# Scale vectors spread by GpSimd instead of the PE, and q of the third batch turned by the PE

## The chip, the cores and the metric

The kernel runs on one core of one Trainium2 chip. The metric is the device time of one execution in microseconds. Engines by the profile's names: PE (TensorE, matrix products, with PEld for its weight loads), DVE (VectorE), ACT (ScalarE), POOL (GpSimd), SP (SyncE, which here only starts DMA transfers). A "q" after an engine's name (ACTq, SPq) means its queue of DMA issues.

## The reference

Grouped attention over 8 batches (16 query heads that share 4 key heads, 384 positions, 64 per head), whose output goes into a residual MLP with per-channel scales:

```python
scores = scale * np.matmul(q, k.transpose(0, 1, 3, 2))      # k, v repeated 4x along heads
attn = softmax(scores)
x = matmul(attn, v)                                         # [8, 384, 1024] after a transpose
a1 = alpha1 * x + beta1
tok = np.einsum('ts,bsd->btd', w_tok, a1)
u = x + lam * tok
a2 = alpha2 * u + beta2
ch = np.maximum(a2 @ w_ch1, 0.0) @ w_ch2                    # 1024 -> 4096 -> 1024
out = u + lam * ch
```

alpha1, beta1, alpha2, beta2 and lam are vectors of 1024 numbers, one for each channel. Where channels lie along the free dimension, the kernel needs each vector copied to all 128 partitions. It keeps four such copies in `vecs`: alpha1 times lam (`g1`), beta1 times lam (`h1`), alpha2 (`al2`) and lam (`lam_t`).

## The kernel before

The eight batches go through a pipeline. `side(b)` is the attention of a batch, the product with w_tok and the turn of the result; `main(b)` is its MLP, in two parts: the first product (`h`, 32 column blocks) and the second (`ch`). The attention of batch b + 1 is cut into pieces and put between the matrix products of `main(b)`, at numbered places (`turns` for the first part, the second dictionary for the second). The attention of batch 0 has nothing to hide behind: it stands alone at the start ("the first batch" below).

```python
        def q_transpose(p, n=2, tag="tp", eng="DVE"):     # PE turns q of two pairs of heads
            src = qrs[1][:, 2 * p:2 * (p + n)] if b else qgs[2 * p // G][...]
            ...
            for i in range(n * NST):
                nc.tensor.matmul(out=ps[:, i, :], lhsT=src[:, i * P:(i + 1) * P], rhs=ident_f if f else ident,
                                 is_transpose=True, ...)
            evac(eng)(out=qT[:, p:p + n].rearrange("p a j s -> p (a j) s"), in_=ps)

        def scores(i, later=False):                       # q k^T, then exp on ACT
            sc = bank([P, 2, 4, P], "sc", "sc") if first else three()
            ...
                if first:                                 # the first batch's exponentials lie in hT
                    e = hTf[:, i % 6 * 1024:(i % 6 + 1) * 1024].rearrange("p (h k s) -> p h k s", h=2, k=4)
                nc.scalar.activation(out=e, in_=sc, func=EXP, scale=scale_qk)

        def av_piece(p, hh):
            ...
            nc.vector.tensor_tensor(out=x[...], in0=av[:, :, :, :D], in1=rinv.to_broadcast([P, 2, NST, D]), op=MUL)
            if first:
                a1s[p] = hTf[:, 6144 + p % 3 * S:6144 + (p % 3 + 1) * S].rearrange("p (a d) -> p a d", a=NST)
                nc.vector.tensor_tensor(out=a1s[p], in0=x[:, :, cols(p)], in1=bc(g1, p), op=MUL)
                return

        def spread(ps_, vs, tag, eng="DVE"):              # PE copies rows to all partitions
            ...
            for i, p in enumerate(ps_):
                nc.tensor.matmul(out=ps[:, i * w:(i + 1) * w], lhsT=sel[:, p:p + 1].to_broadcast([P, P]),
                                 rhs=rows_b[:, vs[0] * P:vs[1] * P], start=True, stop=True)
            evac(eng)(out=vecs[...], in_=...)
```

A float32 row goes through `spread` as three bf16 parts whose sum it is; `split` makes the parts on DVE (a cast, a difference, twice over). In the first batch, `beta1` enters the product with w_tok by a small extra product with two helper matrices `R` and `H` (`rows_r` and `fill_h`), and `fill_h` needs the split row.

The steps of the first batch stand in a table: after scores group i come the listed pieces (`ut` is the turn of the result for the MLP).

```python
        at = {0: [(warmup, 3), (scale_rows, 0), (split, 0, 1, 0)], 1: [(k_transpose, 1, 1), (split, 0, 1, 1)],
              2: [(q_transpose, 2, 2, "av")], 3: [(warmup, 1), (spread, lower, (0, 1), "tp")],
              4: [(av, 0)], 5: [(wtok_transpose, 0, "av"), (wtok_transpose, 1, "tp")],
              6: [(av, 1), (wtok_transpose, 2, "av"), (k_transpose, 2, 2, "tp")], 7: [(q_transpose, 4, 2, "av"), (scale_rows, 1), (split, 1, 2)],
              8: [(fill_h, 0), (rows_r, "tp"), (av, 2)], 9: [(spread, upper, (0, 1), "av", "ACT"), (q_transpose, 6, 2, "mm")],
              10: [(tok, 0)],
              11: [(av, 3)], 12: [(tok, 1), (ut, 0)], 13: [(av, 4), (tok, 2)], ...}
```

Loads: the vectors come from SP's queue, the weights from POOL's (w_ch1 in a ring of five chunks):

```python
        for t in (stage[:, 2120:2824], rows_b, sel):
            nc.vector.memset(t, 0.0)
        load_row(0, moe_alpha1); load_row(3, moe_lam); load_k(0, [2]); load_row(1, moe_beta1) ...
        ...
        load_v(0)
        nc.gpsimd.dma_start(out=wtok_in, ...)
        load_q4(2)
        load_q4(3)
        place_k(0, 0, (0,))
        for c in range(RING):
            load_w1(c)
        place_k(0, 1)          # k of the second pair of key heads to bf16, on POOL
```

The q and k of batch 2 and later are turned by DMA transposes (`flip_k`, `flip_q`), those of batch 2 from ACT's queue late in the first part of `main(1)`:

```python
                moves = [(0, 46 + 4 * i, flip_q, 2, 2 * i - 2, 2) if i else (0, 46, flip_k, 2) for i in range(5)]
```

The softmax here doesn't subtract the row's maximum and nothing guards it: scores larger than these inputs give would overflow.

Of the kernel before, what the change touches and what calls it, by code (L numbers as in the profile page):

```python
# [12 lines left out]
def kernel(  # L13
# [27 lines left out]
    ADD = mybir.AluOpType.add  # L41

# [74 lines left out]
    def flip_queue(b):  # L117
        return nc.scalar if b == 2 else nc.sync

    def flip_k(b):  # L120
        flip_queue(b).dma_start_transpose(out=kT.rearrange("p st h s -> p (st h) s"),
                                    in_=k2s[b].rearrange("p st h a d -> p (st h a d)"))

    def flip_q(b, i=0, n=NP):
        flip_queue(b).dma_start_transpose(out=qT[:, i:i + n].rearrange("p a j s -> p (a j) s"),
                                    in_=qrs[b][:, 2 * i:2 * (i + n)].rearrange("p h st d -> p (h st d)"))
# [16 lines left out]
    def bank(shape, tag, name, dtype=f32):  # L143
        if tag == "mm":
            return mms.tile(shape, dtype, tag="mm", name=name, bufs=2)
        return psum.tile(shape, dtype, tag=tag, name=name, bufs=2 if tag == "sc" else 1)

    def three():
        return threes[0].tile([P, 2, 4, P], f32, tag="sc", name="sc", bufs=3)
# [24 lines left out]
    def side(b):  # L174
# [22 lines left out]
        def q_transpose(p, n=2, tag="tp", eng="DVE"):  # L197
            src = qrs[1][:, 2 * p:2 * (p + n)] if b else qgs[2 * p // G][:, 2 * p % G:2 * p % G + 2 * n]
            src = src.rearrange("p h st d -> p (h st d)")
            f = src.dtype == f32  # L200
            ps = bank([P, n * NST, P], tag, "tp", src.dtype)
            for i in range(n * NST):
                nc.tensor.matmul(out=ps[:, i, :], lhsT=src[:, i * P:(i + 1) * P], rhs=ident_f if f else ident,  # L203
                                 is_transpose=True, start=(i == 0), stop=(i == n * NST - 1), skip_group_check=True)
            evac(eng)(out=qT[:, p:p + n].rearrange("p a j s -> p (a j) s"), in_=ps)
# [33 lines left out]
        def av_piece(p, hh):  # L239
# [20 lines left out]
            if first:  # L260
                a1s[p] = hTf[:, 6144 + p % 3 * S:6144 + (p % 3 + 1) * S].rearrange("p (a d) -> p a d", a=NST)
                nc.vector.tensor_tensor(out=a1s[p], in0=x[:, :, cols(p)], in1=bc(g1, p), op=MUL)
                return
# [3 lines left out]
            nc.vector.tensor_tensor(out=a1s[p], in0=t, in1=bc(h1, p), op=ADD)  # L267

# [40 lines left out]
        def rows_r(tag):  # L309
            ps = bank([P, 512], tag, "r")  # L310
            for st in range(NST):
                nc.tensor.matmul(out=ps[:32, :S], lhsT=ones, rhs=wtokT[:, st, :], start=(st == 0),
                                 stop=(st == NST - 1))
            turned = ps[:, S:S + 2 * NP].rearrange("p (i n) -> p i n", i=2)
            for i, c in enumerate((2, 4)):
                nc.tensor.matmul(out=turned[:, i], lhsT=rows_f[:NP, c * P:(c + 1) * P], rhs=ident_f[:NP, :NP],
                                 is_transpose=True, start=True, stop=True, skip_group_check=True)
            t = hTf[:32, 7296:7296 + S]
            nc.scalar.copy(out=t, in_=ps[:32, :S])
            nc.vector.scalar_tensor_tensor(out=R[:32], in0=t, scalar=masks[2], in1=ps[:32, :S], op0=MUL, op1=ADD)  # L320
            nc.vector.tensor_copy(out=al2T, in_=turned[:, 0])
            nc.vector.tensor_copy(out=a2T[:, :, S:S + 1], in_=turned[:, 1, :, None])


        def spread(ps_, vs, tag, eng="DVE"):
            n = len(ps_)
            ps = bank([P, 4, P], tag, "vec")
            w = vs[1] - vs[0]
            for i, p in enumerate(ps_):
                nc.tensor.matmul(out=ps[:, i * w:(i + 1) * w], lhsT=sel[:, p:p + 1].to_broadcast([P, P]),  # L330
                                 rhs=rows_b[:, vs[0] * P:vs[1] * P], start=True, stop=True)
            evac(eng)(out=vecs[:, vs[0]:vs[1], ps_[0] * P:(ps_[-1] + 1) * P].rearrange("p v (n d) -> p n v d", n=n),
                      in_=ps[:, :n * w].rearrange("p (n v) d -> p n v d", n=n))
# [16 lines left out]
        if not first:  # L350

            turns = {}
            if b == 1:
                turns = {4: [(split, 2, 4, 0)], 8: [(split, 2, 4, 1)], 12: [(k_transpose, 0)],
                         16: [(q_transpose, 0, 2, "av")], 20: [(k_transpose, 2)]}
                for i in range(3):
                    turns[24 + 4 * i] = [(q_transpose, 2 + 2 * i, 2, "av")]
                for i in range(4):
                    turns[34 + 4 * i] = [(spread, (2 * i, 2 * i + 1), (1, 3), "tp", "ACT")]
                for i in range(2):  # L360
                    turns[50 + 4 * i] = [(spread, range(4 * i, 4 * i + 4), (3, 4), "av", "ACT")]
# [10 lines left out]
        lower, upper = range(NP // 2), range(NP // 2, NP)  # L372
        ut = a2_transpose
        at = {0: [(warmup, 3), (scale_rows, 0), (split, 0, 1, 0)], 1: [(k_transpose, 1, 1), (split, 0, 1, 1)],
              2: [(q_transpose, 2, 2, "av")], 3: [(warmup, 1), (spread, lower, (0, 1), "tp")],
              4: [(av, 0)], 5: [(wtok_transpose, 0, "av"), (wtok_transpose, 1, "tp")],
              6: [(av, 1), (wtok_transpose, 2, "av"), (k_transpose, 2, 2, "tp")], 7: [(q_transpose, 4, 2, "av"), (scale_rows, 1), (split, 1, 2)],
              8: [(fill_h, 0), (rows_r, "tp"), (av, 2)], 9: [(spread, upper, (0, 1), "av", "ACT"), (q_transpose, 6, 2, "mm")],
              10: [(tok, 0)],
              11: [(av, 3)], 12: [(tok, 1), (ut, 0)], 13: [(av, 4), (tok, 2)], 14: [(ut, 1), (fill_h, 4), (tok, 3)],  # L380
              15: [(av, 5), (ut, 2)], 16: [(tok, 4), (ut, 3)], 17: [(av, 6), (tok, 5)]}
# [4 lines left out]
        for f, *a in ((ut, 4), (h_part, (0, 1), range(4)), (av, 7), (ut, 5), (tok, 6),  # L386
                      (h_part, (2, 3), range(4)), (h_part, range(4), (4,)), (ut, 6), (tok, 7),
                      (h_part, range(4), (5,)), (ut, 7), (h_part, range(4), (6,)), (h_part, range(4), (7,))):
            add(f, *a)
# [65 lines left out]
    with tc.manual_schedule(engines=order):  # L455
# [12 lines left out]
        rows_f = hTf[:32, 9216:10496].bitcast(f32)  # L468
        rows_t = hTf[:32, 10496:11520].bitcast(f32)
        rows_b = hTf[:, 11520:12032]  # L470
# [10 lines left out]
        sel = stage[:, 2852:2856].bitcast(bf)  # L481
        for t in (stage[:, 2120:2824], rows_b, sel):
            nc.vector.memset(t, 0.0)
# [5 lines left out]
        load_row(0, moe_alpha1)  # L489
        load_row(3, moe_lam)  # L490
        load_k(0, [2])
        load_row(1, moe_beta1)
        load_row(2, moe_alpha2)
        load_row(4, moe_beta2, 1)
# [18 lines left out]
        with nc.allow_low_precision("ones and zeros"):  # L513
            for t, n in ((sel, 24), (sel4, 32)):
                nc.vector.tensor_reduce(out=t[:n], in_=ident[:n, :n].rearrange("p (k c) -> p c k", c=NP), op=ADD, axis=AX)


        def scale_rows(i):
            r = rows_f[:, i * P:(i + 1) * P]
            nc.vector.tensor_tensor(out=r, in0=r, in1=rows_f[:, 3 * P:4 * P], op=MUL)  # L520


        def split(lo, hi, step=None):
            c = slice(lo * P, hi * P)
            for i, m in enumerate(masks[:2]):
                if step in (None, i):
                    src, dst = (rows_t, rows_f) if i else (rows_f, rows_t)
                    nc.vector.tensor_copy(out=rows_b[:32, c], in_=src[:, c])
                    nc.vector.scalar_tensor_tensor(out=dst[:, c], in0=rows_b[:32, c], scalar=m, in1=src[:, c],
                                                   op0=MUL, op1=mybir.AluOpType.subtract)  # L530
            if step != 0:
                nc.vector.tensor_copy(out=rows_b[:32, c], in_=rows_f[:, c])


        def fill_h(p):
            nc.vector.tensor_tensor(out=H[:32, p * P:(p + 4) * P].rearrange("p (n d) -> p n d", n=4),
                                    in0=rows_b[:32, None, P:2 * P].to_broadcast([32, 4, P]),
                                    in1=sel4[:, p:p + 4, None].to_broadcast([32, 4, P]), op=MUL)

        load_v(0)  # L540
        nc.gpsimd.dma_start(out=wtok_in, in_=moe_w_tok.rearrange("(p tt) s -> p tt s", tt=NST))
        load_q4(2)
        load_q4(3)
        place_k(0, 0, (0,))
        for c in range(RING):
            load_w1(c)
        place_k(0, 1)
# [11 lines left out]
        for b in range(B):  # L559
            us = side(b + 1) if b + 1 < B else ({}, {})  # L560


            moves = []
            if b == 1:
                moves = [(0, 46 + 4 * i, flip_q, 2, 2 * i - 2, 2) if i else (0, 46, flip_k, 2) for i in range(5)]
# [41 lines left out]
```

## Time and profile before

| | before |
|---|---|
| time, median of 3 runs | 806.96 us (805.3 to 807.57) |
| span of the profiled run | 803.5 us |
| granted PE clock | 1.00 |
| first batch's lone part | to 38.48 us, when the first `h` product of `main(0)` begins |

In the profile's lines "L410" is the line of the kernel's source, `h<-a2T,w` the tiles written and read. A time line gives start and length in us, the engine, the line, the operation, and in brackets how long the engine sat idle before it and what ended that. A table by stage gives the busy time of each engine in a stretch.

In the first batch these rows of the profile place the parts that the change touches. On PE, the spread of the first half of `g1` at 9.00 us (4 products), of the second at 16.47 (4 products); in `main(0)`, spreads at 60.74, 63.57, 66.40 and 69.23 (2 products each) and at 72.07 and 74.90 (4 each). On DVE, the memsets before the row loads at 1.56 (704 elements, 0.65 us) and 2.21 (256, 0.27). On SP's queue, the issue of alpha1's row at 1.25. On POOL, the casts of `place_k(0, 1)` at 11.42 after five chunk loads at 0.88 each. In `main(1)`, five transposes on ACT's queue from 163.78 to 179.9.

### The profile page before, as it was taken

The numbers are of one execution on the slowest core, as the hardware profiler recorded it, in microseconds if no ns is written. First come the engines' busy times: TensorE is split into PE (matmuls) and PEld (weight loads), VectorE is DVE, ScalarE is ACT, GpSimd is POOL, SyncE is SP. The second block draws the span as 40 slices with busy tenths as digits, with TensorE's granted clock in tenths as the row PEclk, the third lists the DMA queues.
The fourth block names the chain that finished last, engine by engine and source line by source line (L and its number), as shares of the span: only waits on it lengthen the run. The fifth ranks groups of instructions, "written<-read, shape, count | busy, mean of one in ns | idle before, by whom it ended". The sixth has DMA issues, their size and how long they took to land.

```text
span 803.5 us, 14220 instructions
## 1 busy us (share of the span) xinstructions
PE 793.8 (99%) x6123; PEld 452.0 (56%) x6123; DVE 343.5 (43%) x669; ACT 226.9 (28%) x309; POOL 178.5 (22%) x233
## 2 busy tenths in 40 slices
PE   8999999999999999999999999999999999999997
PEld 4766555655556555565555655566555655556545
DVE  8652465215552266322662236622366225552122
ACT  6624431223402233123221233122431223312100
POOL 7234231332013500135002340033400330003000
PEclk9999999999999999999999999999999999999999
DMA  9999999999269972999439991499914995129611
GB/s 190 202 186 202 205 207 170 187 186 170 66 126 188 198 101 58 162 189 196 74 73 169 193 196 43 92 174 197 163 46 114 165 198 88 48 61 187 82 40 40
DMA packets 234975, 113.17 MB, mean 141 GB/s; under 512 B 84376, under 2 KB 228768, under 8 KB 234912
## 3 DMA queue, kind: packets, MB, share of 16 engines
q0 software_dynamic: 170752, 83.47, 79.1%
q1 hardware_dynamic: 58848, 27.22, 13.5%
q10 hardware_dynamic: 5312, 1.57, 1.5%
q8 instruction: 48, 0.79, 0.4%
q14 instruction: 15, 0.12, 0.0%
HBM read 170.53 MB, written 12.58 MB: 228 GB/s over the span
## 4 chain that ended last, share of the span: by engine, by line
PE 84%; DMA 10%; issue 3%; DVE 1%; POOL 1%; ACT 0%; POOLq 0%
PE ch L443 37%; PE h L410 34%; DMA w<-in_moe_w_ch_dram 8%; PE sc L217 4%; PE sc L252 3%; PE sc L273 3%; DMA qT<-q_raw 1%; POOL w L136 1%; PE h L168 1%; PE tok L273 1%; PE av L252 0%; PE warm L460 0%; PE ut L290 0%; PE tp L203 0%; ACT hT L226 0%
## 5 line engine op out<-in xcount | busy, mean ns | idle before, releaser
L443 PE MATMUL ch<-w,hT 128*128 128x512 bf16 (+2 forms) x1600 | 357.7, 371 | 1.1 <-DVE o L448 0.9
L410 PE MATMUL h<-a2T,w 128*128 128x384 bf16 (+1 forms) x2016 | 331.5, 326 | 0.8 <-ACT hT L418 0.8
L410 PEld LDWEIGHTS <-w 128*128 128x128 bf16 x2016 | 196.8, 98 | 131.2 <-issue 1.5
L443 PEld LDWEIGHTS <-hT 128*128 128x128 bf16 x1600 | 144.6, 98 | 153.1 <-issue 10.5
L136 POOL DMA_DIRECT2D w<-in_moe_w_ch_dram x128 | 112.1, 878 | 519.3 <-PE h L410 500.5
L226 ACT ACTIVATE es<-sc 128x1024 bf16<-128x1024 f32 x126 | 121.4, 1023 | 187.9 <-PE sc L217 175.8
L420 DVE TENSOR_SCALAR hT<-h,bias 128x384 bf16<-128x384 f32 x128 | 79.1, 618 | 218.3 <-PE h L410 217.7
L418 ACT ACTIVATE hT<-h,bias 128x384 bf16<-128x384 f32 x128 | 74.3, 580 | 304.9 <-PE h L410 299.4
L448 DVE TENSOR_TENSOR o<-ch,vecs 128x512 f32<-128x512 f32 (+2 forms) x50 | 33.4, 669 | 107.8 <-PE ch L443 107.8
L252 PEld LDWEIGHTS <-es 128*128 128x128 bf16 x1008 | 38.2, 97 | 13.2
L273 PEld LDWEIGHTS <-wtokT 128*128 128x128 bf16 x576 | 37.3, 98 | 13.8 <-DVE x L258 1.7
L217 PE MATMUL sc<-qT,kT 64*128 64x384 bf16 (+2 forms) x576 | 41.9, 272 | 0.7 <-DMA qT<-q_raw 0.6
L257 DVE RECIPROCAL rinv<-sc 128x6 f32<-128x6 f32 x56 | 10.8, 193 | 68.4 <-PE sc L252 67.5
L252 PE MATMUL sc<-v,es 128*128 128x65 bf16 x1008 | 39.9, 193 | 0.0
L280 DVE TENSOR_TENSOR x<-sc,x 128x384 f32<-128x384 f32 x56 | 31.0, 553 | 20.0 <-PE sc L273 20.0
L273 PE MATMUL sc<-a,wtokT 128*128 128x128 bf16 x504 | 37.3, 219 | 0.0
L217 PEld LDWEIGHTS <-kT 64*128 64x128 bf16 x576 | 21.6, 94 | 24.5 <-issue 18.2
L449 DVE TENSOR_TENSOR o<-o,x 128x512 f32<-128x512 f32 (+2 forms) x50 | 33.5, 670 | 1.7
L284 DVE TENSOR_TENSOR a<-x,vecs 128x384 bf16<-128x384 f32 x56 | 32.7, 584 | 1.9
L265 DVE TENSOR_TENSOR a1f<-x,vecs 128x384 f32<-128x384 f32 x56 | 31.2, 558 | 1.9
L267 DVE TENSOR_TENSOR a<-a1f,vecs 128x384 bf16<-128x384 f32 x56 | 31.2, 558 | 1.9
L258 DVE TENSOR_TENSOR x<-sc,rinv 128x384 f32<-128x384 f32 x56 | 31.2, 558 | 1.9
(75 smaller groups left out, 203.1 us busy)
## 6 DMA issues: line engine op xcount, KB each, us to landing
w<-in_moe_w_ch_dram POOLq DMA_DIRECT2D x144, 512.0 KB, 8.6
out_dram<-o SPq DMA_DIRECT2D x47, 256.0 KB, 2.0
q_raw<-in_q_dram POOLq DMA_DIRECT2D x28, 192.0 KB, 8.1
kst<-in_k_dram SPq DMA_DIRECT2D x16, 192.0 KB, 3.4
v<-in_v_dram POOLq DMA_DIRECT2D x24, 64.0 KB, 7.9
a2T<-a SPq DMA_TRANSPOSE x56, 2.3
qg<-in_q_dram POOLq DMA_DIRECT2D x3, 192.0 KB, 5.9
stage<-in_q_dram ACTq DMA_DIRECT2D x2, 192.0 KB, 3.7
```

Of the source, the lines that this page charges most:

```text
L136: nc.gpsimd.dma_start(out=t, in_=w1src[:, :, c * CW * P:(c + 1) * CW * P])
L217: nc.tensor.matmul(out=sc[:, hh, k % 4:k % 4 + n], lhsT=kT[r, sk, 2 * p // G, :], rhs=qT[r, p, st:st + n, :], start=True, stop=True)
L226: nc.scalar.activation(out=e, in_=sc, func=EXP, scale=scale_qk)
L252: nc.tensor.matmul(out=av[:, hh, sq, :], lhsT=ess[k // 4][:, m % 2, k % 4, :], rhs=vb[:, sk, hk, :], start=(sk == 0), stop=(sk == NST - 1))
L273: nc.tensor.matmul(out=ps[:, tt, :], lhsT=wtokT[:, st, tt * P:(tt + 1) * P], rhs=a1s[p][:, st, :], start=(st == 0), stop=(st == NST - 1 an ...
L284: nc.vector.tensor_tensor(out=a2s[p], in0=u, in1=bc(al2, p), op=MUL)
L410: nc.tensor.matmul(out=ps[:, :n], lhsT=w1[:, dt, j * P:(j + 1) * P], rhs=a2T[:, dt, :n], start=(dt == 0), stop=(dt == NDT - 1))
L418: nc.scalar.activation(out=hT[:, nt, :], in_=ps[:, :S], func=RELU, bias=c1)
L420: nc.vector.tensor_scalar(out=hT[:, nt, :], in0=ps[:, :S], scalar1=c1, scalar2=0.0, op0=ADD, op1=mybir.AluOpType.max)
L443: nc.tensor.matmul(out=ps[:, lo:hi], lhsT=hT[:, nt, ms * P:(ms + 1) * P], rhs=w2[:, nt, dw * 512 + lo:dw * 512 + hi], start=(nt == 0), sto ...
L448: nc.vector.tensor_tensor(out=o[:, lo:hi], in0=ps[:, lo:hi], in1=lam_t[:, c], op=MUL)
L449: nc.vector.tensor_tensor(out=o[:, lo:hi], in0=o[:, lo:hi], in1=x[:, ms, c], op=ADD)
```

## The change

It does three things.

The scale vectors are no longer spread by the PE. The rows are loaded as four quarters of 256 numbers onto partitions 0, 32, 64 and 96, scaled by lam on POOL (`scale`), and copied to all partitions by POOL's `partition_broadcast`, in float32 (`broadcast`): for alpha1 times lam in the first batch, for the other three in `main(0)`. The split of beta1, which the extra product still needs, moves from DVE to POOL.

The q of batch 2 is turned by PE for three of its four parts; k and the first part are turned by DMA from SP's queue, at the beginning of `main(1)`.

The first batch is put in another order: the scaling by `g1` is a step of its own (`a1`) and the w_tok product begins later.

```diff
-    def flip_queue(b):
-        return nc.scalar if b == 2 else nc.sync
...
     def flip_k(b):
-        flip_queue(b).dma_start_transpose(...)
+        nc.sync.dma_start_transpose(...)
...
+        def a1(p):
+            a1s[p] = hTf[:, 6144 + p % 3 * S:6144 + (p % 3 + 1) * S].rearrange("p (a d) -> p a d", a=NST)
+            nc.vector.tensor_tensor(out=a1s[p], in0=x[:, :, cols(p)], in1=bc(g1, p), op=MUL)
...
-        def spread(ps_, vs, tag, eng="DVE"):
...
+            turns = {16 + 8 * i: [(q_transpose, 2 + 2 * i, 2, "three")] for i in range(3)} if b == 2 else {}
             if b == 1:
-                turns = {4: [(split, 2, 4, 0)], 8: [(split, 2, 4, 1)], 12: [(k_transpose, 0)],
-                         16: [(q_transpose, 0, 2, "av")], 20: [(k_transpose, 2)]}
+                turns = {12: [(k_transpose, 0)], 16: [(q_transpose, 0, 2, "av")], 20: [(k_transpose, 2)]}
...
-                for i in range(4):
-                    turns[34 + 4 * i] = [(spread, (2 * i, 2 * i + 1), (1, 3), "tp", "ACT")]
-                for i in range(2):
-                    turns[50 + 4 * i] = [(spread, range(4 * i, 4 * i + 4), (3, 4), "av", "ACT")]
+                for i in range(3):
+                    turns[6 + 4 * i] = [(broadcast, 1 + i)]
...
-        at = {0: [(warmup, 3), (scale_rows, 0), (split, 0, 1, 0)], 1: [(k_transpose, 1, 1), (split, 0, 1, 1)],
...
+        at = {0: [(warmup, 3)], 1: [(k_transpose, 1, 1)],
+              2: [(q_transpose, 2, 2, "av")], 3: [(warmup, 1)],
+              4: [(av, 0)], 5: [(a1, 0)], 6: [(av, 1), (k_transpose, 2, 2, "tp")],
+              7: [(q_transpose, 4, 2, "av"), (a1, 1)], 8: [(av, 2)],
+              9: [(wtok_transpose, 0, "av"), (wtok_transpose, 1, "tp")],
+              10: [(wtok_transpose, 2, "av"), (q_transpose, 6, 2, "mm"), (fill_h, 0)], 11: [(av, 3), (rows_r, "tp")],
+              12: [(a1, 2)], 13: [(tok, 0), (av, 4), (a1, 3)],
+              14: [(tok, 1), (ut, 0), (a1, 4)], 15: [(av, 5), (tok, 2), (a1, 5), (fill_h, 4)], 16: [(ut, 1), (tok, 3)],
+              17: [(ut, 2), (av, 6), (a1, 6)]}
...
+        quarters = hTf[:, 9216:11264].bitcast(f32).rearrange("p (v d) -> p v d", v=4)
...
-        for t in (stage[:, 2120:2824], rows_b, sel):
+        for t in (stage[:, 2120:2824], quarters):
             nc.vector.memset(t, 0.0)
...
+        def load_quarters(i, ap):
+            nc.sync.dma_start(out=quarters[0:P:32, i], in_=ap.rearrange("(a d) -> a d", a=4))
+
+        load_quarters(0, moe_alpha1)
+        load_quarters(3, moe_lam)
         load_k(0, [2])
+        load_row(0, moe_lam)
         load_row(1, moe_beta1)
+        load_quarters(1, moe_beta1)
+        load_quarters(2, moe_alpha2)
...
+        def scale(i):
+            q_ = quarters[:, i]
+            nc.gpsimd.tensor_tensor(out=q_, in0=q_, in1=quarters[:, 3], op=MUL)
+
+        def broadcast(i, lo=0, hi=4):
+            for a in range(lo, hi):
+                nc.gpsimd.partition_broadcast(vecs[:, i, a * 256:(a + 1) * 256], quarters[32 * a:32 * a + 1, i])
+
+        def split():
+            ...    # eight small GpSimd operations on beta1's row
...
-        for c in range(RING):
-            load_w1(c)
-        place_k(0, 1)
+        scale(0)
+        broadcast(0, 0, 2)
+        load_w1(0)
+        place_k(0, 1)
+        load_w1(1)
+        split()
+        load_w1(2)
+        broadcast(0, 2, 4)
+        scale(1)
+        for c in range(3, RING):
+            load_w1(c)
...
-                moves = [(0, 46 + 4 * i, flip_q, 2, 2 * i - 2, 2) if i else (0, 46, flip_k, 2) for i in range(5)]
+            moves = [(0, 1, flip_k, 2), (0, 1, flip_q, 2, 0, 2)] if b == 1 else []
```

[...]The built program before has one load of a library (before the identity's affine select); the changed one has six: that one, and one before the first broadcast, the split, the second broadcast, the second `scale` and the broadcasts in `main(0)`.

## The prediction

> **What bounds the kernel now.** I read the page from the top: busy shares, the chain that ended last, then a table by stage, and only then the time line of the stages that the change touches.

> ```profile
> PE 793.8 (99%) x6123; PEld 452.0 (56%) x6123; DVE 343.5 (43%) x669; ACT 226.9 (28%) x309; POOL 178.5 (22%) x233
> ...
> PE 84%; DMA 10%; issue 3%; DVE 1%; POOL 1%; ACT 0%; POOLq 0%
> ```

> The stages (us from the start; then length, and busy us of each engine with its instructions, the granted clock, the DMA share and GB/s):

> ```profile
> 0.00:38.50 38.50, 34.60 (x440) 23.07 (x441) 28.08 (x78) 25.43 (x34) 18.79 (x31) 1.00 1.37 193
> 38.50:78.40 39.90, 39.90 (x278) 25.13 (x277) 16.42 (x41) 15.08 (x38) 16.46 (x21) 1.00 1.37 196
> ...
> 134.70:179.20 44.50, 42.79 (x267) 25.07 (x265) 10.24 (x17) 9.28 (x16) 15.21 (x19) 1.00 1.33 184
> ```

> PE has no idle time to win outside two stages. In the first 38.5 us (batch 0's attention) it is idle for 38.50 - 34.60 = 3.9 us, of which 1.53 is the start. In 134.7 to 179.2 it is idle for 1.71. From 38.5 to 134.7 it never waits, so there only work taken off PE counts. The end (3.6 us) is not touched. So this change can win a few us at best, out of 807: two per cent would be 16. The chain's 10% of DMA is not a PE wait: it is followed back from the one stall below.

> The time line of PE (start, length, line, operation, tiles, count; in brackets the idle time before it and what ended it):

> ```profile
> 7.44 0.39 PE L217 MATMUL sc<-qT,kT 64*128 64x128 bf16 x4
> ...
> 12.66 0.51 PE L192 MATMUL tp<-ident,k 128*128 128x128 bf16 x6 [0.22 <-POOL k L106]
> ...
> 13.93 0.49 PE L203 MATMUL tp<-ident,qg 128*128 128x128 bf16 x6 [0.44 <-DVE wtokT L305]
> ...
> 18.96 0.34 PE L273 MATMUL tok<-hT,wtokT 128*128 128x128 bf16 x3 [1.43 <-DVE x L258]
> ...
> 167.60 2.76 PE L410 MATMUL h<-a2T,w 128*128 128x384 bf16 x16 [0.19 <-ACT hT L418]
> ...
> 178.42 0.83 PE L217 MATMUL sc<-qT,kT 64*128 64x384 bf16 x12 [0.64 <-DMA qT<-q_raw]
> ```

> These are PE's waits: 0.22, 0.44 and 1.43 in the first batch, and around 167 to 178 a row of small ones on ACT, the last on the turned q. ACT shows why:

> ```profile
> 6.36 6.52 ACT L226 ACTIVATE hT<-sc 128x1024 bf16<-128x1024 f32 x7 [0.27 <-PE sc L217]
> ...
> 166.99 2.92 ACTq L125 DMA_TRANSPOSE qT<-q_raw  x1
> 169.96 0.58 ACT L418 ACTIVATE hT<-h,bias 128x384 bf16<-128x384 f32 x1 [2.41 <-PE h L410]
> ```

> Each transpose of batch 2 holds ACT's queue for about 3 us, and the relu behind it comes late: 166.99 + 2.92 = 169.91, and it starts at 169.96 (the bracket names the PE's signal; the queue ahead of it is in the row above). The first line shows the other limit: from 6.36 ACT runs seven exponentials back to back, 6.52 / 7 = 0.93 us each. The third scores group starts at 7.44, just as the first exponential ends.

> [...]The program before loads a library once, ahead of the identity's affine select, and the trace shows no such price: the select starts at 2.44, the memset before it began at 2.14 and took 0.22. But [...]no run yet shows a switch to another. [...]the trace has none of these, only casts of 384 at 0.5 to 0.7 us.[...]

> **The change part by part.**

> Spreads in the middle of batch 0. Six groups leave PE's stream. Each costs the distance from its start to the next start: 60.74 to 60.96 is 0.22 us, likewise at 63.57, 66.40 and 69.23; 72.07 to 72.29 is 0.22, 74.90 to 75.13 is 0.23. Sum 1.33. PE never waits there, so this comes off whole: **-1.33**. What replaces it is 12 broadcasts on GpSimd; from the casts I estimate 0.3 to 0.5 us each for 256 elements, 4 to 6 us in a stage where GpSimd is busy 16.46 of 39.90.

> Third batch's q. The transposes leave ACT's queue, so the waits at 167.60 to 178.42 go: 0.19 + 0.23 + 0.41 + 0.23 + 0.64 = 1.70. k and the first two pairs are turned at the stage's start on SP, when nobody needs them for 40 us. Three groups of six 128x128 transposes come to PE. Such a group costs 0.34 (56.15 to 56.48, for batch 1): 3 x 0.34 = 1.02. The copies to SBUF are 0.56 each on DVE, which has 34 us free. **-0.68**.

> First batch. Removed from PE: two spread groups, 9.00 to 9.33 and 16.47 to 16.71, 0.57. The product with w_tok moves from after the eleventh scores group to after the fourteenth, so that av, scores and turns fill the place of the 1.43 wait. If all three waits went, it would be -0.57 - 2.09 = -2.7. But the changed program also has a new wait. The first exponential writes hT, where the rows lie too, and it now waits for four row loads: alpha1, lam, beta1, alpha2 as quarters. They lie at other columns; the quarters stand in every 32nd partition, and I take the wait to be a cautious one. It is in the order with its waits all the same. When do they land? The first of them waits for the memset of the quarters. Memset: 704 elements took 0.65, so 1024 take 0.95; it starts at 2.21 and ends near 3.2, where alpha1's row was issued at 1.25 before. SP then issues, at its 0.45 to 0.67 each: two quarters, k, two rows, then beta1 and alpha2, until about 6.9. The trace's early loads of k and q need 3.4 to 3.7 us to land; smaller ones I take at 2 to 3. So the first exponential starts at about 9.0 and not at 6.36.

> From there: the third scores group at 9.0 + 1.05 = 10.1 (before 7.44). PE's work from there to the end of the stage was 38.48 - 7.44 = 31.04 less the 2.09 idle, less the 0.57: 28.4. Up to the fourteenth scores group PE has some 9.9 us of it by the rows' start-to-start times, ACT eleven exponentials, 10.2, so ACT sets this part and adds 0.3. The end of the stage: 10.1 + 28.4 + 0.3 = 38.8, against 38.48. Some small wait for DVE will remain: **+0.5**. The stage gets denser, but starts later by as much.

> Sum: +0.5 - 1.33 - 0.68 = -1.5. The rest of the kernel, 620 us of PE, is as before. 807.0 - 1.5 = 805.5.

> **The rivals.**

> First: [...]The built program goes to the broadcast's library and back: five switches more, four of them before the fourth w1 chunk is loaded. For it: [...]that these switches stand in GpSimd's stream between loads and casts that PE needs. Against it: nobody who had seen such a price would have put the halves of one broadcast on both sides of the split of beta1; and the select at 2.44. [...]GpSimd reaches the first scaling at about 7.2 (all loads ahead were issued by 7.09 before); broadcasts end near 15, one w1 issue (0.88) and the casts of k (1.18) near 17, where PE wants them at about 14.4: +2.5. The split ends near 27, DVE's chain behind it near 29, the w_tok product waits: +5 to 7. Two more switches put the last of the five w1 chunks at 43, ten more loads of 0.75 follow, and the sixth chunk is issued near 51 and lands after 7 us or more: PE waits again, some 3 to 8. [...]Together +11 to +23, the other terms -1.5: 817 to 829. At 1 us a switch it all hides, at 2 to 3 us about +1 to +5.

> Second: the wait of the first exponential is shorter than I think ([...]the memset is faster). Then the first batch is up to 2.5 us shorter: 803.

> Third: transposes on SP at 136 us meet the w1 stream, where the DMA share is already 1.33 of the mean. Their lines took 3 us on ACT's queue and 1.24 later on SP. I expect no PE wait from it; at worst one w1 chunk is late, +1.

> **Range and chances.** I give the cheap switch about two chances in three: 803 to 808 then; the dear one nearly one in three, 817 to 829. The number is the first case with a little of the middle one: 806. The range reaches from the second rival to within the first: 801.5 to 826. Faster by over 2% (below 790.8) would need more than PE's whole idle time in the stages touched: 0.01. Slower by over 2% (above 823.1) needs the dear switch with most of its waits: 0.26. Within 2%: 0.73.

> **What would show it.** First exponential at 8.5 to 9.5, waiting on a load, and PE's third scores group 1.05 later: the new wait is right; at 6.4 it is wrong. Main part of batch 0 from 38.5 to 39.5 and 38.6 us long, with no PE wait: the cheap switch. No relu wait at 167 to 178, three groups of q turns of 0.34 in it. If GpSimd shows gaps of several us ahead of the broadcasts, of the split and of the second scaling, and PE waits for the casts of k, for the w_tok product and for a w1 chunk, the first rival holds and my number is 11 to 23 us low. A wait in the later batches would be something that I have not seen.

## The result, and the profile after

The changed kernel takes 846.81 us (median of 4 runs, 845.43 to 848.27) against 806.14 before: ratio 1.0503, 95% interval 1.0477 to 1.0528. It is 5% slower; the prediction was 806.0, with a range that ended at 826.

The page of the changed kernel: busy shares, granted clock in 40 slices, the chain that ended last by engine, and the group of the h products.

```profile
PE 796.5 (94%) x6050; PEld 456.1 (54%) x6117; DVE 339.8 (40%) x652; ACT 223.5 (26%) x302; POOL 191.3 (23%) x259
...
PEclk9788899999999999999999999999999999999999
...
PE 87%; issue 5%; DMA 5%; POOL 2%; DVE 1%; SPq 0%; POOLq 0%
...
L399 PE MATMUL h<-a2T,w 128*128 128x384 bf16 (+1 forms) x2016 | 333.8, 328 | 13.6 <-DMA w<-in_moe_w_ch_dram 13.0
```

PE's busy time is almost the same (793.8 before), but its share falls from 99% to 94%: PE waits. The clock is low only in slices 2 to 5, the first 105 us. "issue" on the chain, time in which an engine waited for nothing that the profile shows, rises from 3% (of 803.5, 24 us) to 5% (of 844.8, 42 us). And one wait of 13.0 us for a w1 chunk stands behind the h group.

By stage (first product of one part of `main` to the first of the next, worked out from the time line; us; the lead is the lone part of the first batch):

| | lead | h of 0 | ch of 0 | h + ch of 1 | span |
|---|---|---|---|---|---|
| before | 38.48 | 39.92 | 55.05 | 99.06 | 803.5 |
| after | 65.22 | 54.72 | 55.28 | 98.53 | 844.8 |

Of the 41.3 us, 26.7 are in the lead and 14.8 in the h part of batch 0. Batch 1 is 0.5 shorter; the stages after it have the lengths of before, 41.60 and 55.05.

The time line of GpSimd in the changed kernel (start, length, line, operation, count; in brackets the idle time before it and what ended it), the rows with a gap:

```profile
10.13 0.28 POOL masks.py:199 TENSOR_SCALAR_AFFINE_SELECT ident<-ident 128x128 bf16<-128x128 bf16 x1 [7.77 <-issue]
...
23.21 0.98 POOL L519 PARTITION_BROADCAST vecs<-hT  x2 [7.53 <-issue]
...
38.07 0.45 POOL L524 TENSOR_TENSOR hT<-hT 32x128 f32<-32x128 f32 x1 [11.17 <-issue]
...
50.89 0.98 POOL L519 PARTITION_BROADCAST vecs<-hT  x2 [7.83 <-issue]
...
58.78 0.87 POOL L515 TENSOR_TENSOR hT<-hT 128x256 f32<-128x256 f32 x1 [6.91 <-issue]
...
73.67 0.88 POOL L134 DMA_DIRECT2D w<-in_moe_w_ch_dram  x1 [0.53 <-PE h L399]
...
83.05 1.80 POOL L519 PARTITION_BROADCAST vecs<-hT  x4 [7.42 <-issue]
```

Six gaps that nothing in the profile explains, 48.6 us together, and they stand exactly where the program loads a library: ahead of the select, and wherever its stream goes from float32 products to a broadcast or back. The first is ahead of the identity's affine select, where the kernel before had none. The row at 73.67 is the issue of the sixth w1 chunk. These are PE's longest waits, from its time line, to be compared with the rows above:

```profile
11.57 0.48 PE L192 MATMUL tp<-ident,k 128*128 128x128 bf16 x3 [6.99 <-DVE k L107]
...
26.14 0.82 PE L192 MATMUL tp<-ident,k 128*128 128x128 bf16 x6 [5.34 <-POOL k L107]
...
44.00 0.29 PE L279 MATMUL tok<-stage 128*128 128x128 bf16 x1 [9.25 <-DVE stage L322]
...
52.90 0.34 PE L275 MATMUL tok<-hT,wtokT 128*128 128x128 bf16 x3 [1.91 <-DVE x L258]
...
86.58 1.47 PE L399 MATMUL h<-a2T,w 128*128 128x385 bf16 x4 [13.02 <-DMA w<-in_moe_w_ch_dram]
```

Each is a piece of GpSimd's stream that came late. DVE's casts of k stand in DVE's queue behind the copies of the identity, so they wait for the select at 10.13 and start at 11.09. The second casts of k stand behind the broadcasts of 23.21 and start at 25.12. R's product (L279) stands behind the split of 38.07. The sixth chunk was issued at 73.67, and PE could go on 12.9 us later, at 86.58. The waits add up to 36.5 us. What runs after some of them runs at a low clock. From the table by stretches (start and end, length, busy us of PE, PE's weight loads, DVE, ACT and GpSimd with their counts, then the granted clock, the DMA share and GB/s):

```profile
26.10:34.70 8.60, 8.56 (x99) 5.27 (x99) 3.91 (x9) 5.77 (x7) 0.80 (x1) 0.71 1.01 141
...
86.60:94.00 7.40, 7.40 (x36) 4.12 (x37) 1.68 (x4) 0.74 (x2) 5.14 (x10) 0.59 1.39 184
```

Here PE is busy throughout, at 0.71 and 0.59.

So my theory after the result was: A, a library load stops GpSimd for about 7 us, and PE waits for what GpSimd then does late; the rest of the change is as good as predicted. The rivals: B, the broadcasts or the small operations on GpSimd are slow in themselves; C, the wait of the first exponential, which I had predicted, is the larger part; D, the low clock after the waits is a cost of its own.

### The profile page after: what moved, and what is told of

It reads as the page before. It is cut to its first block, busy times and chain, and to the rows that moved or that the text cites. A ratio compares the mean times of both kernels' runs of the same rounds, so it can differ in the third digit from the quotient of the medians.

```text
span 844.8 us, 14165 instructions
## 1 busy us (share of the span) xinstructions
PE 796.5 (94%) x6050; PEld 456.1 (54%) x6117; DVE 339.8 (40%) x652; ACT 223.5 (26%) x302; POOL 191.3 (23%) x259
## 4 chain that ended last, share of the span: by engine, by line
PE 87%; issue 5%; DMA 5%; POOL 2%; DVE 1%; SPq 0%; POOLq 0%
PE h L399 38%; PE ch L432 37%; PE sc L217 4%; DMA w<-in_moe_w_ch_dram 4%; PE sc L252 4%; PE sc L275 3%; DMA a2T<-a 1%; PE h L168 1%; POOL w L139 0%; PE tok L275 0%; PE tp L203 0%; POOL v L111 0%; POOL w L134 0%; PE ut L292 0%; DMA hT<-in_moe_lam_dram 0%
## 5 line engine op out<-in xcount | busy, mean ns | idle before, releaser
L432 PE MATMUL ch<-w,hT 128*128 128x512 bf16 (+2 forms) x1533 | 346.0, 370 | 4.6 <-issue 1.1
L432 PEld LDWEIGHTS <-hT 128*128 128x128 bf16 x1600 | 144.7, 98 | 152.8 <-issue 10.2
L226 ACT ACTIVATE es<-sc 128x1024 bf16<-128x1024 f32 x126 | 121.4, 1023 | 187.9 <-PE sc L217 179.1
L275 PEld LDWEIGHTS <-wtokT 128*128 128x128 bf16 x576 | 37.9, 99 | 14.5 <-DVE x L258 2.1
L217 PE MATMUL sc<-qT,kT 64*128 64x384 bf16 (+2 forms) x576 | 43.3, 278 | 1.5 <-ACT hT L226 0.5
L217 PEld LDWEIGHTS <-kT 64*128 64x128 bf16 x576 | 21.7, 95 | 25.1 <-issue 19.9
L258 DVE TENSOR_TENSOR x<-sc,rinv 128x384 f32<-128x384 f32 x56 | 31.2, 558 | 1.9
```

What stands on the lines that cost most here:

```text
L217: nc.tensor.matmul(out=sc[:, hh, k % 4:k % 4 + n], lhsT=kT[r, sk, 2 * p // G, :], rhs=qT[r, p, st:st + n, :], start=True, stop=True)
L275: nc.tensor.matmul(out=ps[:, tt, :], lhsT=wtokT[:, st, tt * P:(tt + 1) * P], rhs=a1s[p][:, st, :], start=(st == 0), stop=(st == NST - 1 an ...
L432: nc.tensor.matmul(out=ps[:, lo:hi], lhsT=hT[:, nt, ms * P:(ms + 1) * P], rhs=w2[:, nt, dw * 512 + lo:dw * 512 + hi], start=(nt == 0), sto ...
```

## The experiments

**Switches alone.** The kernel before, with an unused broadcast and an unused float32 product in the ch parts of batches 2, 3 and 4, where GpSimd has time.

```diff
+    def there_and_back():
+        nc.gpsimd.partition_broadcast(scratch, lam_t[0:1, :256])
+        nc.gpsimd.tensor_tensor(out=scratch, in0=scratch, in1=scratch, op=MUL)
...
+            if 2 <= b <= 4:
+                moves += [(1, 24, there_and_back)]
```

> The kernel before, plus one broadcast of 256 elements and one float32 product of 256 into a scratch tile, unused, in the second product of batches 2, 3 and 4, where GpSimd has nothing to do: six switches that nobody waits for. Theory A: before each of the six operations GpSimd stands still for about 7 us beside an idle DMA (7.0 to 7.9 in five of the six places of the changed kernel), and the span stays within 1 us of 803.5. Rival: a switch is cheap (under 1 us) and the gaps of the changed kernel are waits for transfers; then no gap here. The broadcast itself: 0.4 to 0.55 us.

The first pair in GpSimd's time line of this kernel:

```profile
289.97 0.55 POOL L85 PARTITION_BROADCAST scratch<-vecs  x1 [6.28 <-issue]
...
297.27 0.60 POOL L86 TENSOR_TENSOR scratch<-scratch 128x256 f32<-128x256 f32 x1 [6.75 <-issue]
```

The six gaps are 6.16 to 7.12 us; the operations themselves take 0.55 to 0.60. The time stays, 806.52 against 806.68 before (one run). The span is 804.7, 0.2 above what A allowed and within the 803.6 to 805.5 of the runs of before: here, where nobody waits for GpSimd, a switch is free. A's price is shown apart from everything else of the change, and B falls for single operations. A switch to the broadcast took 6.2 to 6.8, one back 6.8 to 7.1, and every one was paid, not only the first.

**Two loads in place of six.** The changed kernel, with its work on GpSimd sorted by library: both scalings and the split, then all broadcasts.

```diff
         scale(0)
-        broadcast(0, 0, 2)
-        load_w1(0)
         place_k(0, 1)
-        load_w1(1)
-        split()
-        load_w1(2)
-        broadcast(0, 2, 4)
+        load_w1(0)
         scale(1)
-        for c in range(3, RING):
+        split()
+        load_w1(1)
+        broadcast(0)
+        for c in range(2, RING):
             load_w1(c)
```

> The changed kernel with its GpSimd work in one order that needs two library loads in place of six: scaling and split first, then all broadcasts. Theory A: four switches of 7 to 11 us go, but the load ahead of the identity stays (7 us of PE waiting) and the w_tok product waits for the one broadcast at about 32 us: first batch ends at 50 to 56, no PE wait for a chunk of w_ch1 in the first product of batch 0 (before: 13.0), time 816 to 824. Theory B: about as the changed kernel, 840 to 847, since the same operations are done in the same places for PE.

Measured: 823.66 us, ratio 1.0212 (1.0195 to 1.0229), lead 58.54, h of batch 0 38.60. GpSimd's gaps in it, from its time line:

```profile
10.37 0.28 POOL masks.py:199 TENSOR_SCALAR_AFFINE_SELECT ident<-ident 128x128 bf16<-128x128 bf16 x1 [8.02 <-issue]
...
31.29 2.07 POOL L519 PARTITION_BROADCAST vecs<-hT  x4 [8.03 <-issue]
```

and PE's:

```profile
11.81 0.48 PE L192 MATMUL tp<-ident,k 128*128 128x128 bf16 x3 [7.24 <-DVE k L107]
...
34.22 0.60 PE L217 MATMUL sc<-qT,kT 64*128 64x384 bf16 x4 [11.43 <-DVE qT L205]
```

Four loads fewer, and the order that allows it, are worth 22.9 us of span (844.8 - 821.9), with the same operations on the same engine: A, and not B. The edit can't part the loads from the order; that four gaps are gone is what the time line shows. The time is in A's range; the lead was 2.5 us longer than expected, because all of alpha1's broadcasts now wait for one late load. DVE's first product with them stands ahead of the copies of k and q that PE needs, in DVE's time line:

```profile
31.87 0.67 DVE L269 TENSOR_TENSOR hT<-x,vecs 128x384 bf16<-128x384 f32 x1 [12.18 <-POOL vecs L519]
...
33.61 0.55 DVE L205 COPY qT<-tp 128x768 bf16<-128x768 bf16 x1
```

The h part is at the length predicted for the change.

**One library.** The library that has both the select and the broadcast is loaded at the start, and the float32 products and the split, for which the program loads the other one, go to DVE. Six steps of the lead are put ahead of them in program order, and the split and beta1's product with lam behind the eighth scores group.

```diff
+        nc.gpsimd.load_library(library_config._reserved_1)
...
-            nc.gpsimd.tensor_tensor(out=q_, in0=q_, in1=quarters[:, 3], op=MUL)
+            nc.vector.tensor_tensor(out=q_, in0=q_, in1=quarters[:, 3], op=MUL)
...
     def split():    # likewise, six operations on nc.vector in place of eight
...
+        begin = side(0)
+        for f in begin[:6]:
+            f()
```

> The changed kernel with everything kept that it does for speed, but no switch of GpSimd's library: the broadcast's library is loaded once at the start (it also holds the affine select) and the scaling and the split go back to VectorE. Theory A (each switch stops GpSimd for 7 to 11 us, and PE waits for what stands behind it; nearly all of the 41 us): no gap on GpSimd, the first batch ends at 38.5 to 40 us, the first product of batch 0 takes 38.6, time 804 to 807. Theory B (the broadcasts themselves, the new order of the first batch and its late row loads cost the time, the switches only lie beside it): the first batch still ends after 55 us and the time stays above 830.

Measured: 810.84 us, ratio 1.0057 (1.0042 to 1.0072). No such gap is left on GpSimd, and the h part is 38.60. But the lead is 46.94 and the time above the 804 to 807 that A expected. ACT's time line:

```profile
13.40 2.85 ACT L226 ACTIVATE hT<-sc 128x1024 bf16<-128x1024 f32 x3 [6.86 <-DMA kst<-in_k_dram]
```

and the stretches after it (busy us of PE, PE's weight loads, DVE, ACT, GpSimd with their counts, then granted clock, DMA share, GB/s):

```profile
8.00:14.50 6.50, 0.43 (x9) 0.28 (x7) 0.36 (x1) 1.09 (x2) 6.50 (x11) 0.72 1.24 179
14.50:20.00 5.50, 5.50 (x57) 3.07 (x57) 1.87 (x4) 4.71 (x6) 3.36 (x5) 0.50 1.41 207
```

The predicted wait of the first exponential is there, and far longer: 13.40, not 9.0. The load that the row names is a guess of the profile, for no k load is read by an exponential. The last two of the four quarter loads were issued at 6.50 and 7.07, the last by this row of SP's queue:

```profile
7.07 0.53 SPq L482 DMA_DIRECT2D hT<-in_moe_alpha_dram  x1
```

The next two runs ask whether they are it, and what the half clock of the second stretch costs.

**Quarters apart.** The same with the quarters in the room of the other a2T, which nothing writes until they are spread.

```diff
-        quarters = hTf[:, 9216:11264].bitcast(f32).rearrange("p (v d) -> p v d", v=4)
+        quarters = a2Ts[1].rearrange("p n s -> p (n s)")[:, :2048].bitcast(f32).rearrange("p (v d) -> p v d", v=4)
```

> The kernel with one library, but the quarters of the scale vectors lie in a tile of their own instead of in hT, so that the first exponential, which writes hT, no longer waits for four small loads. Theory A (this wait, and the low clock that follows it, are nearly all that is left of the loss): the first exponential starts at 6.0 to 6.8 us instead of 13.40, no PE wait of over 1 us before 20 us, lead 38 to 40.5 us instead of 46.94, main(0) h part 38.6, time 802 to 804.5. Theory B (the new order of the lead, with w_tok's product and the splits later, costs by itself): the first exponential is early, but the wait moves to w_tok's product and grows, lead 42 to 45, time 806 to 809.

ACT in this kernel, from its time line:

```profile
6.19 4.69 ACT L226 ACTIVATE hT<-sc 128x1024 bf16<-128x1024 f32 x5 [0.26 <-PE sc L217]
```

PE's longest wait in it:

```profile
17.62 0.33 PE L304 MATMUL tp<-ident,stage 128*128 128x128 bf16 x3 [2.33 <-DVE wtokT L307]
```

The exponential starts at 6.19 and PE's wait for it is gone: lead 39.76, 7.2 us shorter for the place of one tile, with the same loads issued at the same times (6.49 and 7.07). Time 804.02 us, ratio 0.9969 (0.9957 to 0.9980): this version is 0.3% faster than the kernel before. One point missed A: a wait of 2.33 us before 20 us was not expected.

**Its wait filled.** The one-library kernel, quarters still in hT, with 30 more warm-up products ahead of the third scores group.

```diff
-        at = {0: [(warmup, 3)], 1: [(k_transpose, 1, 1)],
+        at = {0: [(warmup, 3)], 1: [(k_transpose, 1, 1), (warmup, 30)],
```

> The kernel with one library, with 30 warm-up products in the wait for the first exponential (the quarters still lie in hT). Theory A (the clock is a cost beside the wait: TensorE idle for 6 us is granted half speed for the next 6): the exponential still starts at 13 to 14, but the granted clock from 14.5 to 20 us is 0.85 or more instead of 0.50, the lead falls by 2 to 3 to 44 to 45, time 807.5 to 809. Theory B (the clock falls for another reason, or what follows waits for the exponentials anyway): lead 46.5 to 47.5, time 810 to 811.5.

The stretch behind the wait, and ACT's time line in it:

```profile
14.50:20.00 5.50, 4.70 (x82) 3.02 (x82) 3.39 (x8) 5.48 (x7) 3.33 (x5) 1.00 1.41 209
```

```profile
12.62 7.57 ACT L226 ACTIVATE hT<-sc 128x1024 bf16<-128x1024 f32 x8 [6.30 <-issue]
```

The clock is full, as A said. The lead is 46.09, between the two (A to 45, B from 46.5): 0.85 shorter, of which 0.78 is the exponential's earlier start (12.62 against 13.40). Time 811.29, ratio 1.0063 (1.0049 to 1.0078), as B said: no gain, since batch 1 takes 98.40 and not 97.73. Behind the wait ACT runs eight exponentials without a pause; PE at full clock only waits for them. The run also rules out that the first exponential waits for the broadcasts, which read the quarters. GpSimd's last two in the lead start at 12.27 and take 0.95 us (12.29 and 0.96 in the one-library kernel), so they end at 13.22, after the exponential's start at 12.62.

**Quarters apart, loads kept.** The one-line edit above in the changed kernel.

> The changed kernel with the quarters in a tile of their own, nothing else. Theory A (the first library load, which holds back the casts of k, hides the wait for the quarters): lead within 1 us of 65.2, time 845 to 848. Theory B (the wait for the quarters adds to it): lead shorter by 3 to 7, time 839 to 843.

Measured: 845.07 us, ratio 1.0477 (1.0463 to 1.0490), lead 64.76, 0.5 below the changed kernel's. A holds: what shortens the lead by 7.2 us without library loads hardly shortens it with them. In the changed kernel PE's turn of k, and with it the first scores, is itself held until 11.57. C falls for the changed kernel.

**Four waits filled.** The changed kernel with 36, 27, 48 and 67 more warm-up products, placed in PE's four longest waits (ahead of the first turn of k, of the third, of the first product with w_tok, and of the sixth chunk of the h part).

```diff
-        warmup(9)
+        warmup(9 + 36)
...
+              6: [(av, 1), (warmup, 27), (k_transpose, 2, 2, "tp")],
...
+              13: [(warmup, 48), (tok, 0), (av, 4), (a1, 3)],
...
+            if b == 0 and c == RING:
+                warmup(67)
```

> The changed kernel with its six library loads, but with warm-up products of nobody's use in TensorE's four longest waits (36, 27, 48 and 67 of them, some 85% of each wait at 0.163 us), so that TensorE isn't idle in them. Theory A (the low clock after each wait is a term of its own, worth 6 to 8 us by the shares of time at 0.59, 0.71 and 0.90): the clock of the page stays at 9 or more in all slices, time 838 to 842. Theory B (what runs at a low clock is followed by the next wait, which then only grows): 844.5 to 848 although the clock is full.

The clock on its page:

```profile
PEclk9999999999999999999999999999999999999999
```

PE's waits in it:

```profile
42.95 0.34 PE L275 MATMUL tok<-hT,wtokT 128*128 128x128 bf16 x3 [1.99 <-DVE x L258]
...
52.10 0.34 PE L275 MATMUL tok<-hT,wtokT 128*128 128x128 bf16 x3 [3.54 <-DVE x L258]
...
125.78 1.89 PE L434 MATMUL ch<-w,hT 128*128 128x512 bf16 x8 [0.76 <-DMA w<-in_moe_w_ch_dram]
```

844.00 us (843.84 to 844.13), ratio 1.0463 (1.0449 to 1.0478): 2.8 less than the changed kernel, between the two theories. By stages: the lead 65.94 against 65.22, nothing won; the wait at 52.10 grew from 1.91 to 3.54. The h part 49.88 against 54.72, 4.8 won; ch 56.70 against 55.28, 1.4 given back in waits for weights. Of the 4.8, 1.9 is that the sixth chunk came sooner: PE goes on with the h products at 85.27, 11.2 us after the last one, and not 13.0. Another 2.8 come behind it (30.55 to the end of the part, against 33.36), where PE waits in neither kernel, so I put them down to the clock, 1.00 in the 7.4 us behind that wait and 0.59 in the changed kernel. So D is worth about 3 us, in the one place where PE itself is the limit behind its wait.

**The third batch's q alone.** The kernel before, with the transposes taken from ACT's queue and three groups turned by PE.

```diff
-        return nc.scalar if b == 2 else nc.sync
+        return nc.sync
...
+            turns = {16 + 8 * i: [(q_transpose, 2 + 2 * i, 2, "three")] for i in range(3)} if b == 2 else {}
...
-                moves = [(0, 46 + 4 * i, flip_q, 2, 2 * i - 2, 2) if i else (0, 46, flip_k, 2) for i in range(5)]
+            moves = [(0, 1, flip_k, 2), (0, 1, flip_q, 2, 0, 2)] if b == 1 else []
```

> The kernel before with one part of the change alone: q of the third batch turned by PE for three of four parts, the rest by DMA from the sync queue. As predicted: the waits of 1.70 us at 167 to 178 us go and three groups of 0.34 us come, so from the first product of batch 1 to the end of its second 98.4 us in place of 99.1 (in the changed kernel 98.5, with one new wait of 0.58 us), time 805 to 807. Rival: the transposes on the sync queue hold back the weights' transfers, and the stretch is as long as before or longer.

Measured: 805.56 us, ratio 0.9990 (0.9975 to 1.0005), too small for the whole time. The stage shows it. PE's time line there:

```profile
156.55 0.50 PE L205 MATMUL tp<-ident,q_raw 128*128 128x128 bf16 x6
156.88 20.53 PE L412 MATMUL h<-a2T,w 128*128 128x384 bf16 x124
```

A group of turns takes 0.33 to the next start, and the h products run for 20.5 us without one of the waits of before. h + ch of batch 1 takes 97.87 us against 99.06, shorter than the 98.4 expected.

**Rows first.** The best version, with beta1's split in DVE's idle time ahead of its first work on an av product, its rows loaded first, and beta1's product with lam (the expectation calls it alpha2's) in the h part.

```diff
+        load_row(0, moe_lam)
+        load_row(1, moe_beta1)
         load_quarters(0, moe_alpha1)
...
-              2: [(q_transpose, 2, 2, "av")], 3: [(warmup, 1)],
+              2: [(q_transpose, 2, 2, "av")], 3: [(warmup, 1), (split,)],
...
-              7: [(q_transpose, 4, 2, "av"), (a1, 1), (split,), (scale, 1)], 8: [(av, 2)],
+              7: [(q_transpose, 4, 2, "av"), (a1, 1)], 8: [(av, 2)],
...
+                turns[4] = [(scale, 1)]
...
-        broadcast(0, 0, 2)
         load_w1(0)
         place_k(0, 1)
+        broadcast(0, 0, 2)
```

> The kernel with one library and the quarters apart, with beta1's split in VectorE's idle 2 us at 8.7 instead of at 14.2 (its two row loads issued first for that), alpha2's product moved to the h part of batch 0, and the first broadcast behind the first w1 load and the casts of k. Theory A (VectorE's work at 14 to 17 us makes the 2.33 us wait for w_tok's copies): this wait falls under 0.7, lead 38 to 38.8, time 802 to 803.5. Theory B (the rows land after 10 us and stall VectorE, or the later broadcast holds the scaling of x back): lead 39.5 to 42, time 804 to 806.

PE's waits behind the lead in this kernel, which the version above doesn't have:

```profile
45.92 0.83 PE L400 MATMUL h<-a2T,w 128*128 128x385 bf16 x4 [0.70 <-DMA w<-in_moe_w_ch_dram]
85.14 1.89 PE L433 MATMUL ch<-w,hT 128*128 128x512 bf16 x8 [0.41 <-DMA w<-in_moe_w_ch_dram]
...
133.85 0.32 PE L400 MATMUL h<-a2T,w 128*128 128x384 bf16 x1 [0.84 <-DMA a2T<-a]
```

The wait for w_tok's copies falls from 2.33 to 0.26 and the lead to 36.88, 2.9 us shorter and better than A expected. But the time is 803.91, ratio 0.9969 (0.9956 to 0.9983): the same as the version above, and just over the 803.5 at which A's range ended. The next stages give 2.6 of it back: h of batch 0 39.48 (+0.88), ch 55.51 (+0.46), h + ch of batch 1 99.00 (+1.26). The waits that the rows show, 1.95 us of it, are all for transfers: for weights and for a2T. Whether a later order of the loads would keep the 2.9 was not tried.

## Why the prediction was wrong

| kernel | lead | h of 0 | h + ch of 1 | span |
|---|---|---|---|---|
| before | 38.48 | 39.92 | 99.06 | 803.5 |
| after | 65.22 | 54.72 | 98.53 | 844.8 |
| quarters apart, loads kept | 64.76 | 53.61 | 98.60 | 843.9 |
| four waits filled | 65.94 | 49.88 | 98.55 | 842.1 |
| two loads | 58.54 | 38.60 | 98.62 | 821.9 |
| one library | 46.94 | 38.60 | 97.73 | 809.3 |
| one library, quarters apart | 39.76 | 38.60 | 97.74 | 802.1 |

The lead varies by 1 us between programs whose steps in it are the same: 38.48 in the kernel before, and 39.52 and 39.46 in the runs with switches alone and with q alone.

1. The step that failed is the cost of a library switch, which the sum left out: "I give the cheap switch about two chances in three". The first rival, the dear switch, is what happened, with every wait that the prediction named for it. The runs show its price: 6.2 to 7.1 us in a quiet stage, and 6.9 to 11.2 in the changed kernel. I set it aside on two arguments. That nobody would place a broadcast so if it were dear is an argument about people. That the select at 2.44 paid nothing was read wrongly: that program used one library only, and I took a load without a gap for evidence about price. With one library, loaded at the start, the select again pays nothing: it starts at 2.53, after a memset of 0.22 us from 2.23. In the changed kernel, which ends in the broadcast's library, it pays 7.77, and in the one with two loads, which ends there too, 8.02. The kernel with switches alone switches six times, but ends in the ordinary library, and its select pays nothing:

```profile
2.63 0.30 POOL masks.py:199 TENSOR_SCALAR_AFFINE_SELECT ident<-ident 128x128 bf16<-128x128 bf16 x1 [0.28 <-POOL ident masks.py:197]
```

So it is not the number of libraries in a program. These runs sort by the library in which the program ends; what one execution leaves to the next was not measured.

2. The size, within that rival: "+11 to +23". By its terms:

| wait of PE | predicted | measured |
|---|---|---|
| first select | at most the rest of the +23 | 6.99 |
| casts of k | 2.5 | 5.34 |
| w_tok product and what follows it | 5 to 7 | 9.25 + 1.91 |
| sixth w1 chunk | 3 to 8 | 13.02 |

All four are under-sized. The price of a switch in the predicted terms was an assumption that no run had shown. I also worked from a GpSimd that starts on time, but the delays add up along one queue. I had the sixth chunk issued near 51; it was at 73.67. Ahead of it GpSimd stood still for 7.8 us at the first select, which the 51 left out, for 33.4 in the next four gaps, and for 4.7 in waits for other transfers and PE just ahead of the issue. Then 12.9 us passed until PE could go on, not 7. The gap ahead of the split is 11.17, and 10.42 and 10.11 in the two other kernels with this order (quarters apart with the loads kept, four waits filled), about 3 us above the others; why stays open.

3. The clock was not in the prediction. In the run with one library it was 0.50 in the 5.5 us behind a wait of 6.07 us, and 1.00 there with the wait filled. By the lengths of its products it stayed at half until about 21 us, 6.5 after PE had gone on at 14.48: six turns of k at 20.35 took 0.83 us, six of q at 21.43 took 0.51. But filling the waits of the changed kernel gave 2.8 us of 41, and nothing in the lead (65.94 against 65.22). In the one-library kernel with its wait filled ACT was the next limit, with eight exponentials in 7.57 us while PE was busy for 4.70 of 5.50: there a slow PE only shortens its own next wait.

4. The first batch, "+0.5", with the exponential at 9.0: the mechanism was right, and the landing was mis-sized. "Smaller ones I take at 2 to 3" was set against early loads. Issued at up to 7.07, while bulk loads run, they hold the exponential until 13.40, about 6 us. This costs 7.2 us of lead by itself (one library, quarters in hT or apart), but 0.5 in the changed kernel, where the first switch hides it. So the cheap switch would not have given the 803 to 808 of the prediction either: the version without switches that keeps this wait takes 810.84. It is a property of the first layout, and one line removes it. Without it the lead is 39.76, about that of before: the denser order, with the split on DVE, has a wait of 2.33 us for DVE where before had 1.43, and moving the split took it away.

5. The spreads in `main(0)`, "-1.33": 39.92 to 38.60 is -1.32, in every version in which no chunk is late. Twelve broadcasts of 256 elements cost GpSimd 1.77 for each four, 0.44 each, inside the estimate of 0.3 to 0.5.

6. The third batch's q, "-0.68": measured -1.20 alone and -1.32 in the best version. The three groups on PE cost what was said, 0.33 to 0.34 each; the stall was mis-sized. I summed the waits that the time line shows, 1.70. The stage's length shows more: 99.06 - 41.60 - 55.05 = 2.41 against the later batches. The h part alone has 42.25 of PE's busy time against 41.60 in the next batch, with the same products, so my estimate from these two is that some 0.6 us of small waits between products is counted as busy. 2.41 - 1.02 = 1.39 would have been nearer.

7. The third rival, transposes on SP that meet the w1 stream, cost nothing that the runs show. The kernel with q alone and the one with quarters apart have the same transposes at 136.51 and 138.08, and at 135.49 and 137.06, and PE has no wait of over 0.2 us in batch 1. The one wait of the changed kernel there, 0.58 us for a2T, ends at 176.95, before the first of them is issued at 177.31.

The two PE parts of the prediction, -1.33 and -0.68, came to about -2.6 and are what makes the best version 0.3% faster. Nearly the whole error of the changed kernel lies in the engine that was to do the removed work.

## What to carry to other kernels

Before work goes to another engine, count what that engine must load to do it (6.2 to 11.2 us a switch here): sort its operations by library, keep to one library if there is one that holds all of them, and look for gaps that the profile calls "issue" ahead of the first operation after each load (48.6 us in the changed kernel). When an engine stops, everything behind it in its queue comes late (here the sixth w1 chunk, issued at 73.67), so follow each late load or cast to the engine that waits for it, and add the delays along the queue. When a tile is partly written by small late loads, the tile's other writers may wait for them (here an exponential, at 13.40 and not 6.19); a place of its own can be worth more than the work that was saved.
